# Two blocks more per round take the seven-product second layer, and the side steps are spread over less of a round

## The chip, the cores and the metric

The kernel runs on one core of a Trainium2 chip. The metric is the device time of one launch in microseconds. Each core has five engines that run their own instruction streams in order and meet through semaphores: TensorE (PE in the profile, with its weight loads as PEld), VectorE (DVE), ScalarE (ACT), GpSimd (POOL) and SyncE (SP), which here only starts transfers. All of the arithmetic is in float32, and a program's float32 matmul shows up in the trace as two matmul records.

## The reference, cut to what matters

Two stages follow each other. The first is a Fourier mixing of 8 batches of 2496 rows with 256 columns; the second sends each of the 19968 resulting rows to one of 8 experts, a two-layer network.

```python
X = np.fft.fft(np.fft.fft(x, axis=1), axis=2).real          # x: (8, 2496, 256)
x = X.reshape(B * S, D)                                     # 19968 rows of 256
expert_idx = np.argmax(x @ w_gate, axis=1)                  # 8 experts
gate_w = softmax(x @ w_gate)[arange, expert_idx]
for e in range(E):                                          # rows sorted by expert
    h = np.maximum(x_sorted[lo:hi] @ w1[e], 0.0)            # (rows,256) @ (256,1024)
    y_sorted[lo:hi] = h @ w2[e]                             # (rows,1024) @ (1024,256)
return gate_w[:, None] * y
```

## The kernel before, in words

The program is one long list of instructions that Python generators write out in an order fixed at build time. There are two kinds of work.

*Side work* makes the mixed rows of a batch. `first(b)` (L325) folds x on VectorE and multiplies on TensorE (the tiles named `s`), then the result goes through DRAM (`Td`); `second(b)` (L361) multiplies again (tiles `p` and `zz`), makes the finished `rows` on VectorE (L408, L410), and `route` (L416) finds each row's expert and its place in the DRAM table `Xs`. `send` (L462) moves 128 rows at a time into `Xs` with an indirect DMA that GpSimd issues (L236). `mixed(b)` (L882) weaves `first` of one batch with `second` of the one before it, and one step of that generator is a "side step".

*Expert work* is `experts` (L701), which takes blocks of 512, 256 or 128 rows of one expert in the order of `in_order` (L161). `fetch_rows` and `fetch_weights` (L526, L541) bring rows and both weight matrices through SP's queue, up to three blocks ahead. `turn` (L576) transposes the rows of the next block while the present block is in its second layer. A block has a first layer into `hT` (hidden units on partitions) and a second layer from `hT` to the output rows `y`, scaled by the gate on ScalarE and written to `out` by an indirect DMA of GpSimd, 128 rows each.

There are eight rounds, one for each batch. Rounds 3 to 6 (counted from 0) have five 512-row blocks each; round 7, the last, has five of 512 rows, seven of 256 and 21 of 128, the last ones only if they are needed.

Two of the layers are made in a form that replaces eight quarter-size products by seven and some sums of quarters. `seven` (L598) does so for the first layer of every 512-row block from round 3 on and of round 7's 256-row blocks (`halved`, L191). Its stationary side needs three sums of quarters of w1 and one in place (`Left`, L551, one sum per `step`), its moving side those of the transposed rows (`right`, L567). For each half of its work it makes products 0, 5, 6, 4, 1, 3, 2 into the PSUM banks a, b, d, c, a, e, c; after each, VectorE adds the bank to a running sum (L621, L624, L627, L635, L639), and ScalarE applies the Relu. The last product accumulates into bank c, so it has to wait until L627 has read that bank.

`lower` (L645) does the same for the second layer. Its stationary side is quarters and sums of quarters of `hT`: VectorE makes four sums for each half (L780, queued as `chores`), and its moving side is quarters of w2 with three sums and one in place (`below`, L593). In the kernel before only round 7's blocks use it (`quartered`, L196). For a 512-row block `below` runs on GpSimd in one go, while the block before is in its second layer; for a 256-row block it runs on VectorE at the end of the block before. All other blocks have the ordinary second layer (L828): for each 128 rows eight matmuls with 256 columns, which the trace shows as 16.

How the two kinds are mixed is set at L943 to L971. Each `yield` of `experts` gives a weight `w` and a flag. Where the flag is false (only in second layers, from round 3 on), a credit grows by `ticks * w / (SHARE * open_)`, with 32 ticks and `open_` 40 for five blocks; each whole credit runs one side step at that place in the list. With `SHARE` 0.8 the 32 steps are spread over the first four fifths of the round's second layers. `send` has its own pace (L968). A round ends when all steps of its batch have run.

Every engine takes its instructions strictly in the order of this list, so a VectorE instruction that waits holds up all later ones of that engine, whether they belong to side steps or to experts.

Of the kernel before, what the change touches and what calls it, by code (L numbers as in the profile page):

```python
# [12 lines left out]
F32 = mybir.dt.float32  # L13
# [171 lines left out]
SHARE, EARLY, ROOM = 0.8, 0.7, 1.2  # L185
# [10 lines left out]
def quartered(b, size):  # L196

    return halved(b, size) and b == B - 1
# [17 lines left out]
def kernel(ctx: ExitStack, tc, x, w_gate, w1, w2, out):  # L216
# [261 lines left out]
    def plan(b, size, k, last):  # L478
# [3 lines left out]
        def one(name, *dims, dt=F32):  # L482
            return cp.tile([1, *dims], dt, tag="p_" + name, name="p_" + name, bufs=2)
# [109 lines left out]
    def below(w, eng):  # L593

        ws2 = sp.tile([128, 3, FC // 2, H], F32, tag="t4", name="ws2")
        return right(ws2, *(w[:, 4 * f:4 * f + 4, k * H:(k + 1) * H] for f in (1, 0) for k in range(2)), eng=eng)

    def seven(size, l, r, hT, step, after):  # L598
# [13 lines left out]
        for g in range(half // fp):  # L612
            a, b, c, d, e = (pse.tile([128, fp, th], F32, tag=k, name=k) for k in "abcde")
            p1, u2, u3 = (bp.tile([128, fp, th], F32, tag=n, name=n, bufs=1) for n in ("p1", "u2", "u3"))
            h11, h12, h21, h22 = (hT[:, k * half + g * fp:k * half + (g + 1) * fp, t * th:(t + 1) * th]
                                  for k in range(2) for t in range(2))
            product(g, 0, a)
            act.copy(p1[:], a[:])
            yield
            product(g, 5, b)  # L620
            vec.tensor_tensor(u2[:], p1[:], b[:], op=add)  # L621
            yield
            product(g, 6, d)
            vec.tensor_tensor(u3[:], u2[:], d[:], op=add)  # L624
            yield
            product(g, 4, c)
            vec.tensor_tensor(h22, u3[:], c[:], op=add)  # L627
# [7 lines left out]
            vec.tensor_tensor(h21, u3[:], e[:], op=add)  # L635
            act.activation(h21, h21, ACTF.Relu)
            yield
            product(g, 2, c, False)
            vec.tensor_tensor(h12, u2[:], c[:], op=add)  # L639
            act.activation(h12, h12, ACTF.Relu)  # L640
            after(h11, h12, h21, h22, slice(g * fp, (g + 1) * fp))
# [3 lines left out]
    def lower(size, l, r, y, gate, send_rows, step):  # L645
# [14 lines left out]
        def scaled(k, lo, hi, src=None):  # L660
            for i in range(k * nt, (k + 1) * nt):
                act.activation(y[:, i, lo:hi], y[:, i, lo:hi] if src is None else src[:, i - k * nt], ACTF.Copy,
                               scale=gate[:, i])

        p1, u2, u3 = (bp.tile([128, nt, H], F32, tag=n, name=n, bufs=1) for n in ("p1", "u2", "u3"))
        a, b, c, d = (bank(k) for k in "abcd")
        one, two = y[:, nt:2 * nt], y[:, 0:nt]
        product(0, a)
        act.copy(p1[:], a[:])
# [4 lines left out]
        scaled(1, 0, H, a)  # L674
        step()
        yield
        product(5, c)
        vec.tensor_tensor(u2[:], p1[:], c[:], op=add)
        yield
        product(6, d)  # L680
        vec.tensor_tensor(u3[:], u2[:], d[:], op=add)
        vec.tensor_tensor(two[:, :, 0:H], u3[:], b[:], op=add)
        step()
        yield
        c = bank("c")
        product(4, c)
        vec.tensor_tensor(two[:, :, H:], u3[:], c[:], op=add)
        vec.tensor_tensor(u2[:], u2[:], c[:], op=add)
        scaled(0, 0, D)
        send_rows(0, nt)  # L690
# [4 lines left out]
        vec.tensor_tensor(one[:, :, H:], u2[:], d[:], op=add)  # L695
        scaled(1, H, D)
        send_rows(nt, 2 * nt)
        step()
        yield

    def experts(todo):  # L701
# [4 lines left out]
        xbs, got, xT, used, left, rest = [], [], None, None, None, None  # L706
# [30 lines left out]
        for k, (b, size, last, at) in enumerate(todo):  # L737
# [30 lines left out]
            both = quartered(b, size)  # L768
            if both:
                th, r2 = size // 2, rest  # L770
                s12 = xp.tile([128, 2, FC // 2, th], F32, tag="xq", name="s12", bufs=3)
                s4 = xp.tile([128, FC // 2, th], F32, tag="xq", name="s4", bufs=3)
                l2 = [hT[:, 4 * f:4 * f + 4, t * th:(t + 1) * th] for t, f in ((1, 1), (1, 0))]
                l2 += [s4, hT[:, 0:4, 0:th], s12[:, 0], s12[:, 1], hT[:, 4:8, 0:th]]

            def after(h11, h12, h21, h22, at):
                if both:
                    for o, p, q, op in ((s12[:, 0, at], h21, h11, add), (s12[:, 1, at], s12[:, 0, at], h22, sub),
                                        (h21, h22, h21, sub), (s4[:, at], h12, s12[:, 1, at], sub)):
                        chores.append(lambda o=o, p=p, q=q, op=op: vec.tensor_tensor(o, p, q, op=op))  # L780

            if halved(b, size):
                for _ in seven(size, left.all, xT, hT, step, after):
                    yield 0.5, True
                while chores:
                    step()
# [16 lines left out]
            if follow:  # L803
# [9 lines left out]
                if follow[1] == BIG and quartered(*follow[:2]):  # L813
                    rest = below(got[0][1], pool)
            if both:
                y = xp.tile([128, BIG // 128, D], F32, tag="t1", name="y4")

                def send_rows(lo, hi):
                    for i in range(lo, hi):
                        put_row(out, ro[:, i:i + 1], y[:, i], NT - 1, "out")  # L820

                for i, _ in enumerate(lower(size, l2, r2, y, meta[:, :, 1:2], send_rows,
                                            left.step if follow and halved(*follow[:2]) else lambda: None)):
                    if i in (0, 2, 4):
                        xT = next(turned, xT)
                    yield 1, False
# [200 lines left out]
```

## Time and profile before

| What | Value |
|---|---|
| Time, median of 3 runs | 1272.84 us (1270.5 to 1274.08) |
| Profiled execution: its own time | 1280.92 us |
| Profiled execution: span from first to last instruction | 1279.1 us |
| Start of the first seven-product block (round 3) | 349.4 us |
| Start of round 7 | 921.1 us |
| Busy in the span: PE / DVE / ACT / POOL | 1221.0 / 700.4 / 436.3 / 398.3 us |

The span is that of the profiled execution alone; 1.8 us of its time lie outside of it, and it took 8.1 us longer than the median of the runs without a profile. Times in microseconds of the trace count from the start of the span. The five 512-row blocks of a round start (first product of `seven`) at 495.7, 528.9, 556.5, 586.2 and 616.1 us in round 4, and the next round starts at 642.0. The fifth has no side steps and takes 25.9 us; the others are longer by the TensorE time of the side steps in them.

### The profile page before, as it was taken

The page shows a single profiled execution, that of the slowest core. Times are in us where ns is not written, and L with a number is a line of the kernel's source. Part 1 is how long each engine was busy: PE and PEld are TensorE (multiplying, and loading weights), DVE is VectorE, ACT ScalarE, POOL GpSimd, SP SyncE. Part 2 cuts the span into 40 slices and gives each one's busy share as a digit, 9 for nine tenths or more (in the row PEclk, how much of TensorE's full clock was granted, in tenths as well). Part 3 has the DMA queues.
Part 4 walks back from the last instruction along what each step waited for, and adds up shares of the span by engine and source line. Part 5 has one row for each costly group of instructions (what it writes and reads, how often), then busy time and mean ns, then how long its engine had stood idle before and what let it go on. Part 6 is the DMA issues. An engine that isn't in the chain of part 4 may idle for free.

```text
span 1279.1 us, 21208 instructions
## 1 busy us (share of the span) xinstructions
PE 1221.0 (95%) x6905; PEld 1077.0 (84%) x6905; DVE 700.4 (55%) x1772; ACT 436.3 (34%) x1096; POOL 398.3 (31%) x495
## 2 busy tenths in 40 slices
PE   6768999999999999999999999999999999999996
PEld 4557898876788888888888888888889999999995
DVE  4455434343466655564556455674578774444662
ACT  1423332332243433434343343432333332222232
POOL 0235327145116311561116411461453321111112
PEclk6859999999999999999999999999999999999998
DMA  8859798765348553573336434443435238778786
GB/s 241 279 181 321 242 339 297 204 228 175 125 146 260 162 153 113 175 240 114 104 118 211 144 120 149 132 152 107 130 121 167 91 129 296 283 277 276 280 279 246
DMA packets 163211, 249.72 MB, mean 195 GB/s; under 512 B 118601, under 2 KB 130227, under 8 KB 143516
## 3 DMA queue, kind: packets, MB, share of 16 engines
q1 hardware_dynamic: 146327, 203.28, 50.0%
q0 software_dynamic: 15888, 42.14, 9.1%
q10 hardware_dynamic: 885, 2.94, 0.7%
q8 instruction: 56, 0.92, 0.3%
q14 instruction: 55, 0.45, 0.1%
HBM read 194.91 MB, written 54.83 MB: 195 GB/s over the span
## 4 chain that ended last, share of the span: by engine, by line
PE 87%; DMA 6%; DVE 3%; another core or an unknown queue 2%; issue 1%; ACT 1%; SPq 0%; POOL 0%; POOLq 0%; DVEq 0%; ACTq 0%
PE py L221 32%; PE ph L221 10%; PE c L221 10%; PE a L221 10%; PE p L221 6%; PE d L221 6%; PE b L221 5%; PE e L221 4%; PE s L221 3%; DMA xq<-in_x_dram 2%; DMA Td<-t 1%; DMA t<-Td 1%; DMA xb<-Xs 1%; PE rk L221 0%
## 5 line engine op out<-in xcount | busy, mean ns | idle before, releaser
L221 PE MATMUL py<-w_sb,hT 128*128 128x256 f32 x2016 | 454.9, 380 | 1.3 <-DVE hT L796 1.3
L221 PEld LDWEIGHTS py<-w_sb,hT 128*128 128x128 f32 x2016 | 377.6, 190 | 51.2 <-DVE hT L796 1.7
L236 POOL DMA_INDIRECT out_dram<-y,ro x163 | 160.4, 984 | 694.0 <-ACT y L837 482.6
L236 POOL DMA_INDIRECT Xs<-rows,pi x160 | 163.2, 1020 | 109.9 <-DVE rows L410 52.1
L221 PE MATMUL ph<-xT,w_sb 128*128 128x128 f32 (+2 forms) x992 | 171.3, 328 | 6.1 <-DVE hT L796 3.3
L221 PEld LDWEIGHTS ph<-xT,w_sb 128*128 128x128 f32 x992 | 135.5, 192 | 30.5 <-issue 17.9
L837 ACT ACTIVATE y<-py,xb 128x256 f32<-128x256 f32 x129 | 61.0, 473 | 239.5 <-PE py L221 213.0
L221 PE MATMUL a<-xT,w_sb 128*128 128x256 f32 (+1 forms) x512 | 117.5, 356 | 0.0
L621 DVE TENSOR_TENSOR u<-p,b 128x512 f32<-128x512 f32 x57 | 39.1, 687 | 124.2 <-PE b L221 95.0
L796 DVE TENSOR_SCALAR hT<-ph 128x512 f32<-128x512 f32 x43 | 29.7, 690 | 129.5 <-issue 79.2
L221 PEld LDWEIGHTS a<-xT,w_sb 128*128 128x128 f32 x512 | 89.5, 190 | 10.7 <-DVE xT L582 0.4
L408 DVE COPY lg<-p 128x16 f32<-128x16 f32 x80 | 13.9, 174 | 141.5 <-ACT zs L405 121.3
L631 ACT ACTIVATE hT<-a 128x512 f32<-128x512 f32 x57 | 34.0, 597 | 149.5 <-PE a L221 115.7
L585 ACT ACTIVATE xT<-xT 128x256 f32<-128x256 f32 (+1 forms) x94 | 36.4, 387 | 121.8 <-DVE xT L582 71.9
L221 PE MATMUL s<-xq,w 104*112 104x256 f32 (+2 forms) x208 | 62.6, 426 | 11.0 <-DVE xq L297 10.9
L221 PEld LDWEIGHTS p<-table,t 120*128 120x128 f32 x352 | 55.2, 206 | 15.0 <-ACT zz L379 5.5
L221 PE MATMUL p<-table,zz 128*128 128x145 f32 (+1 forms) x320 | 57.2, 304 | 7.6 <-ACT t L321 5.5
L221 PE MATMUL p<-table,t 120*128 120x120 f32 (+1 forms) x352 | 57.7, 291 | 6.1 <-ACT zz L379 4.1
L221 PE MATMUL c<-xT,ws 128*128 128x256 f32 (+1 forms) x256 | 59.5, 359 | 3.2 <-DVE hT L627 3.2
L469 POOL CAST pi<-due 128x1 int32<-128x1 f32 x140 | 39.5, 282 | 69.1 <-ACT due L468 68.7
L582 DVE STREAM_TRANSPOSE xT<-xb 128x512 f32<-128x512 f32 (+1 forms) x94 | 58.2, 625 | 4.3 <-DMA xb<-Xs 4.3
L798 ACT ACTIVATE hT<-ph 128x512 f32<-128x512 f32 x55 | 32.8, 597 | 80.2 <-PE ph L221 64.9
(146 smaller groups left out, 1798.1 us busy)
## 6 DMA issues: line engine op xcount, KB each, us to landing
w_sb<-in_moe_w_dram SPq DMA_DIRECT2D x132, 1024.0 KB
xq<-in_x_dram SPq DMA_DIRECT2D x24, 896.0 KB
xb<-Xs SPq DMA_DIRECT2D x112, 128.0 KB
Td<-t SPq DMA_DIRECT2D x18, 448.0 KB
t<-Td SPq DMA_DIRECT2D x8, 768.0 KB
t<-Td SPq DMA_DIRECT2D x8, 640.0 KB
xb<-Xs SPq DMA_DIRECT2D x52, 64.0 KB
xb<-Xs SPq DMA_DIRECT2D x100, 32.0 KB
```

What stands on the lines that cost most here:

```text
L221: nc.tensor.matmul(o, lhsT=lhsT, rhs=rhs, start=start, stop=stop, **kw)
L236: return unordered(pool.indirect_dma_start(out=dst, out_offset=bass.IndirectOffsetOnAxis(ap=idx, axis=0), in_=rows, in_offset=None, bounds ...
L408: vec.tensor_copy(lg[:, k:k + 2], p3[:, NY:NY + 2 * E].rearrange("p (m e) -> p m e", m=2))
L469: pool.tensor_copy(idx, due[:])
L582: vec.transpose(free(xT[:], 256 * h, [32, n // 32], [BIG, 2], [1, 32]), free(xb, 512 * h, [64, n // 32], [1, 2], [2, 32]))
L585: act.activation(odd, odd, ACTF.Copy, scale=-1.0)
L621: vec.tensor_tensor(u2[:], p1[:], b[:], op=add)
L631: act.activation(h11, a[:], ACTF.Relu)
L796: vec.tensor_scalar(o, ph[:], 0.0, None, op0=ALU.max)
L798: act.activation(o, ph[:], ACTF.Relu)
L837: act.activation(y[:], py[:], ACTF.Copy, scale=meta[:, i, 1:2])
```

## The change

The second layer by sevens is extended to the fourth and fifth blocks of rounds 3 to 6 (`at >= 3`), so that eight blocks more use `lower`. What comes with it:

- `Below` replaces `below`. It hands out its four sums one per `step`. For a fourth block it is started a block early: one sum before each of the four row tiles of the third block's second layer, on GpSimd. Every other block that needs it makes its sums in its own first layer, one at each of the first four products: 512-row blocks on GpSimd, 256-row blocks on VectorE. The tile `ws2` has one buffer.
- `seven` keeps its running sums in `hT` itself instead of the tiles p1, u2, u3, and, where the block goes on to `lower`, leaves out the Relu of the quarter h21.
- The four sums of `hT` are made otherwise: two per half in `seven` (`scalar_tensor_tensor`, which takes the Relu of h21 along), and then s2 and s4 inside `lower`, in place, after its products 0 and 1 have read the old values.
- `lower` keeps its running sums in the `y` tiles, which are now two rows of tiles each with three buffers (before six of one row), also for the ordinary blocks; it reads bank b later, after product 4, and has an eighth, empty `yield`.
- `SHARE` goes from 0.8 to 0.6: the 32 steps fall in the first three fifths of a round's second layers. In the built program they stand in the first three blocks, but for one pair in the fourth block's `lower`.
- Most small tiles of `plan` have one buffer.

```diff
-SHARE, EARLY, ROOM = 0.8, 0.7, 1.2
+SHARE, EARLY, ROOM = 0.6, 0.7, 1.2
...
-def quartered(b, size):
-
-    return halved(b, size) and b == B - 1
+def quartered(b, size, at):
+
+    return halved(b, size) and (b == B - 1 or at >= 3)
...
+    class Below:
+        def __init__(self, w, eng):
+            ws2 = bp.tile([128, 3, FC // 2, H], F32, tag="ws2", name="ws2", bufs=1)
+            o = [ws2[:, k] for k in range(3)]
+            b11, b12, b21, b22 = (w[:, 4 * f:4 * f + 4, k * H:(k + 1) * H] for f in (1, 0) for k in range(2))
+            self.eng, self.all = eng, (b11, b21, b22, o[2], o[0], o[1], b12)
+            self.due = deque([(o[0], b12, b11), (o[1], b22, o[0]), (o[2], b21, o[1]), (b12, b12, b22)])
+
+        def step(self):
+            if self.due:
+                o, p, q = self.due.popleft()
+                self.eng.tensor_tensor(o, p, q, op=sub)
...
             product(g, 0, a)
-            act.copy(p1[:], a[:])
+            act.copy(h11, a[:])
             yield
             product(g, 5, b)
-            vec.tensor_tensor(u2[:], p1[:], b[:], op=add)
+            vec.tensor_tensor(h12, h11, b[:], op=add)
...
             product(g, 3, e)
-            vec.tensor_tensor(h21, u3[:], e[:], op=add)
-            act.activation(h21, h21, ACTF.Relu)
+            vec.tensor_tensor(h21, h21, e[:], op=add)
+            if not both:
+                act.activation(h21, h21, ACTF.Relu)
...
+        p1, u2, u3, high = (y[k][:, 0:nt, h * H:(h + 1) * H] for k, h in ((1, 0), (1, 1), (0, 0), (0, 1)))
         product(0, a)
-        act.copy(p1[:], a[:])
+        act.copy(p1, a[:])
+        s2()
...
         product(1, a, False)
+        s4()
+        step()
+        turn_some()
+        yield
+        product(5, c)
+        vec.tensor_tensor(u2, p1, c[:], op=add)
         scaled(1, 0, H, a)
...
-                    for o, p, q, op in ((s12[:, 0, at], h21, h11, add), (s12[:, 1, at], s12[:, 0, at], h22, sub),
-                                        (h21, h22, h21, sub), (s4[:, at], h12, s12[:, 1, at], sub)):
-                        chores.append(lambda o=o, p=p, q=q, op=op: vec.tensor_tensor(o, p, q, op=op))
+                    part = parts[g]
+                    for o, q, op in ((s1, h11, add), (h21, h22, sub)):
+                        chores.append(lambda o=o[:, part], p=h21[:, part], q=q[:, part], op=op:
+                                      vec.scalar_tensor_tensor(o, p, 0.0, q, op0=ALU.max, op1=op))
...
-                for _ in seven(size, left.all, xT, hT, step, after):
+                for _ in seven(size, left.all, xT, hT, both, step, ends):
+                    if both:
+                        below.step()
                     yield 0.5, True
...
-                if follow[1] == BIG and quartered(*follow[:2]):
-                    rest = below(got[0][1], pool)
+                if not both and size == follow[1] == BIG and quartered(*follow[:2], follow[3]):
+                    soon = Below(got[0][1], pool)
...
+                def s2():
+                    for part in parts:
+                        vec.tensor_tensor(h22[:, part], s1[:, part], h22[:, part], op=sub)
+
+                def s4():
+                    for part in parts:
+                        vec.tensor_tensor(h12[:, part], h12[:, part], h22[:, part], op=sub)
...
-            for i in range(n):
+            for i in range(0 if both else n):
+                if soon:
+                    soon.step()
                 xT = next(turned, xT)
...
-            if follow and follow[1] == BLK and quartered(*follow[:2]):
-                rest = below(got[0][1], vec)
```

## The prediction

> **What bounds the kernel now.** I read the page first, then the table of stages, then who waited for whom, then the order of events in the stages that the change touches. Engine shares and the row of forty slices:
>
> ```profile
> span 1279.1 us, 21208 instructions
> PE 1221.0 (95%) x6905; PEld 1077.0 (84%) x6905; DVE 700.4 (55%) x1772; ACT 436.3 (34%) x1096; POOL 398.3 (31%) x495
> ...
> PE   6768999999999999999999999999999999999996
> ```
>
> TensorE is the bound on average, but what counts is the stages that change. The table of stretches (length, then busy time of PE, PEld, DVE, ACT, POOL, clock) for rounds 3 and 6, then for the fifth block of round 6 and the first two blocks of round 7:
>
> ```profile
> 349.40:495.70 146.30, 146.30 (x742) 129.73 (x741) 85.34 (x204) 57.50 (x141) 45.68 (x60) 1.00 0.53 164
> 786.50:921.10 134.60, 134.60 (x660) 118.91 (x659) 81.17 (x206) 48.61 (x116) 50.86 (x64) 1.00 0.43 137
> ...
> 895.20:921.10 25.90, 25.90 (x122) 22.80 (x121) 13.15 (x22) 8.43 (x16) 9.31 (x8) 1.00 0.40 122
> 921.10:945.80 24.70, 24.70 (x170) 23.10 (x169) 18.80 (x32) 8.19 (x16) 12.13 (x10) 1.00 0.47 139
> 945.80:971.80 26.00, 24.82 (x171) 23.02 (x170) 20.04 (x36) 8.98 (x19) 12.44 (x11) 1.00 0.44 138
> ```
>
> Rounds 3 and 6 have PE busy for their whole length at full clock; rounds 4 and 5 read the same, and from 349 to 921 us the list of PE's waits is empty. So each microsecond of PE work taken away there is one off the end, unless a new wait takes its place. The last three rows are the trial of the change that this trace already holds: the same first layer with an ordinary second layer takes 25.90 us, with the second layer by sevens 24.70, and with one stall in it 26.00. The gain per block is small enough for one stall to eat it.
>
> **Part 1, the products.** TensorE's order of events shows both second layers of a 512-row block:
>
> ```profile
> 907.28 13.98 PE L221 MATMUL py<-w_sb,hT 128*128 128x256 f32 x64
> 921.09 1.03 PE L221 MATMUL a<-xT,w_sb 128*128 128x256 f32 x4
> ...
> 933.25 1.95 PE L221 MATMUL a<-w_sb,hT 128*128 128x128 f32 x16
> ...
> 943.96 1.95 PE L221 MATMUL d<-w_sb,s 128*128 128x128 f32 x16
> ```
>
> The ordinary one runs from 907.28 to 921.09: 64 records in 13.81 us, 216 ns each. By sevens it starts at 933.25 and the next block at 945.75: 7 x 16 = 112 records in 12.50 us, 111.6 ns each. That is 1.31 us less per block (seven eighths of 13.81 would be 1.73 less; the rest is the 3% that a half-width record takes over half). Eight blocks: 8 x 1.31 = 10.5 us off PE.
>
> A rule of the Trainium skill speaks against this. TensorE: Matmul & The Clock Gate, section Back-to-back issue gap, says that in a stream of weight loads and matmuls both set the spacing, so that narrow matmuls are dearer than their columns: 81 ns sustained at 128 columns where 56 stand for one alone, 1.46 times. Taken over, the half-width record would take 1.46 x 108 = 158 ns, the layer 112 x 158 = 17.7 us, and eight blocks would lose 8 x 3.9 = 31 us (an estimate from that page). The row has 112 ns for just this shape with its weight loads beside it, so I use the row.
>
> **Part 2, the waits in a block by sevens.** The new VectorE work per block, counted in the built order: four `scalar_tensor_tensor`, four sums for s2 and s4, six of 128x256 for the banks of `lower`; some 8 us in a 512-row block. At its fifth place in round 6 VectorE had 13.15 of 25.90 us busy, so there is room; what can hurt is order. In round 7 the price shows as a wait, and in its cause:
>
> ```profile
> PE c L221 <- DVE hT L627: 3.2, 5, 1.2
> ```
>
> ```profile
> 955.42 1.29 POOL L570 TENSOR_TENSOR ws<-w_sb 128x512 f32<-128x512 f32 x1
> ...
> 956.79 1.26 POOL L571 TENSOR_TENSOR ws<-w_sb,ws 128x512 f32<-128x512 f32 x1
> ...
> 957.58 0.69 DVE L627 TENSOR_TENSOR hT<-u,c 128x512 f32<-128x512 f32 x1
> 958.14 1.27 POOL L572 TENSOR_TENSOR ws<-w_sb,ws 128x512 f32<-128x512 f32 x1
> 958.18 1.77 DVE L780 TENSOR_TENSOR s<-s,hT 128x512 f32<-128x512 f32 x1
> ```
>
> The first is the list of waits (total, times, longest), the second the order of events in the block of 26.00 us: its second half's h22 sum (L627) came late, and the last product of the first layer waited 1.18 us. GpSimd's weight sums run beside VectorE there, and an L780 sum that lasts 0.68 us otherwise lasts 1.77.
>
> SBUF — State Buffer, section SBUF: two separate sides, gives the reason and a harsher price: GpSimd and a VectorE operation with two SBUF inputs take one port pair in turn, each for its whole instruction, and the other fully blocks. The trace agrees on which: stretched are only sums from SBUF (0.92 to 1.77 us), those with a PSUM bank stay at 0.69. By the rule the two sums of that kind amid GpSimd's four would each wait a full 1.3 us in the fifth blocks, 2.6 us per block against 0.8 us of slack (h22's sum ends at 10.4 us in an undisturbed block, product 2 is due at 11.2): 1.8 x 4 = 7.2 us. In the trace five such sets cost PE 1.18, 0.1 and otherwise nothing, 0.26 each; the bad one began 9.6 us into its block, the others at 2 to 7. In the fifth blocks they begin when GpSimd has sent off the fourth block's rows, near 5.5 us. I take 0.2 x 4 = 0.8 us, between 0 and 7.2. The fourth blocks' sets run in the third block's second layer, where the built order gives VectorE about 13 us of work in 19.
>
> **Part 3, the fourth blocks.** In rounds 3 to 5 the last two side steps land in the fourth block's `lower`, on VectorE between s2 and s4. Walk, with zero at the block's first product; sums of 512 columns follow each other in 0.62 us (seven of them from 934.17 to 937.90). The first layer's last sum starts at 12.3; it and four more end at 15.4; then lg and rows 0.8, the folds 0.7 and 0.95, seven small ones of `route` 1.4: 19.3; s4 twice 1.25, a w1 sum 0.6, a transpose 0.7, the sum that empties bank c 0.4: 22.2. TensorE: first layer 12.1, products 0, 3, 1, 5, 6 at 1.79 each and 0.9 of side work: product 4 wants bank c at 22.0. A stall of 0.2; if each operation is taken at its full 0.68 and small gaps are added, 1.5. I take 0.4 x 3, and 0.1 for round 6: 1.3 us. Late next would be the w2 sums of `y` and, behind them, bank d for the next block's third product, with 0.5 us to spare.
>
> **Part 4, the pacing.** Steps per unit of second-layer weight go from 32/(0.8 x 40) = 1.0 to 32/(0.6 x 40) = 1.33. Nothing is gained by it directly, as PE has no gap there. Round 1 ran at 32/(0.7 x 32) = 1.43, and PE's waits between 200 and 242 us are one of 2.1 us, for a transfer of `Td`. Two steps in a row show there:
>
> ```profile
> 226.65 0.60 PE L221 MATMUL p<-table,t 120*128 120x120 f32 x4
> 227.36 0.74 PE L221 MATMUL p<-table,zz 128*128 128x145 f32 x4
> ```
>
> The second follows 0.71 us after the first instead of 0.44. One such pair per round stands in the new order: 0.3 x 4 = 1.2 us (0 to 2.1 each). The transfer of `Td` is issued at least a block before its first reader, as the built order shows, so I add nothing for it. The sends into `Xs` end before the third block's second layer, so no round starts later.
>
> **Part 5, round 7.** The 512-row blocks keep their count of VectorE sums. In the 256-row blocks the w2 sums move from the block before into the first layer, one before each running sum. Of the 3.2 us of waits above 2.0 lie in four of these seven. Walk: VectorE is through with the rows at 1.1 us; w2 sum, h12, w2 sum, h21, w2 sum, then h22 from 4.5 to 5.2, and product 2 is due at 5.36: that wait goes. Then w2 sum, two sums of banks, two of s1 and h21, and s2 ends at 9.1, when product 5 is due at 8.9: 0.2 x 7 = 1.5 us. Net −0.5 us (−2.0 to +3). A Relu less per half is ScalarE's, which is 34% busy: nothing. The `y` tiles, now three of two rows, are written again a block or more later: nothing.
>
> **The sum.** −10.5 + 0.8 + 1.3 + 1.2 − 0.5 = −7.7 us, on the profiled execution's 1280.92 us (1279.1 of span and 1.8 around it): 1273.2. That execution lies 8.1 us over the median of the runs, 1272.84, and nothing in this sum scales with that: 1265.1 us for the median.
>
> **Rivals.** *The new stalls eat most of it.* The fourth blocks' order at its dear end (1.5 x 3), fifth blocks at 0.6 each and the pacing at 2.4 give −10.5 + 4.5 + 2.4 + 2.4 = −1.2; between that and the forecast, about −3: 1270. For it: VectorE has 19 to 20 of 25 us busy in such blocks and must take side steps too. Against: four of the five in round 7 hardly stall.
> *All covers hold.* No stall in the eight blocks and half of round 7's waits gone: −10.5 − 1.6 = −12.1, 1260.7. For it: the block at 921 us with its 24.70. Against: the walk of the fourth blocks ends with nothing to spare.
> *Slower.* GpSimd's sums meet the first layer's last sums in each fourth and fifth block as they did at 955 us: the price was 26.00 − 24.70 = 1.30 us, so eight times that is 10.4 us and the gain is gone; it decides from a mean stall of 1.31 us per block. With the walk's 1.5 in three blocks on top, −10.5 + 10.4 + 4.5 + 1.2 − 0.5 = +5.1: 1278. For it: the start of GpSimd's sums hangs on when its queue is through with the rows, and that moved by 4 us within five blocks. Against: the fourth blocks' sums are a block early.
> *It does nothing* would need PE to have had gaps in rounds 3 to 6; it has none.
>
> **How the numbers follow.** Forecast 66% (1261.5 to 1268.5), all covers hold 12%, most eaten 14%, slower 8%. The range leaves out half of the second case, a third of the third and the fourth: 1260.0 to 1270.5. A difference under 0.3%, 3.8 us (1269.0), can't be told from none here: faster has the first two and a third of the third, 0.82; slower by as much (over 1276.7) takes half of the last, 0.05; 0.13 between.
>
> **What would show it.** Right: the fifth blocks of rounds 3 to 6 at about 24.8 us from first product to next first product; no PE wait on VectorE over 1.5 us between 349 and 890 us; 112-ns records in the new layers; round 7's waits for h22 gone in 256-row blocks and small ones before product 5. Wrong: PE waiting for s2, for bank c or for bank d in the fourth blocks; PE waiting for `zz` or `oh` in the first three blocks of a round; GpSimd's sums late enough for PE to wait for them.

## The result, and the profile after

The changed kernel takes 1265.8 us (median of 6 runs, 1264.2 to 1270.37), the kernel before on the same chip 1273.46 (6 runs, 1270.5 to 1275.89): ratio 0.995, 95% interval 0.9933 to 0.9967. That is 7.7 us less, as forecast; the parts of the sum, though, came out otherwise than it says, and two of its errors cancel. From one set of runs to the next the median of the kernel before lay between 1272.6 and 1284.1 us, so below a time counts only as a ratio to the kernel before of its own set, or stage by stage.

The head of the page of the changed kernel. The profiled execution is the longest of the six runs (1270.37 us):

```profile
span 1268.5 us, 22212 instructions
PE 1212.5 (96%) x7289; PEld 1083.6 (85%) x7289; DVE 773.6 (61%) x1884; ACT 421.5 (33%) x1087; POOL 445.7 (35%) x527
```

PE has 8.5 us less to do in 384 more records, and the span is 10.6 us shorter. Of these, 2.5 us lie before round 3 (it starts at 346.9 us, not 349.4), which is no effect: the same early rounds ended anywhere between 343.4 and 356.1 us in the runs below. From the first block of round 3 to the end it is 921.6 us after 929.7. The table of stretches, rounds 3, 6 and 7's 512-row blocks, then the third, fourth and fifth block of round 3 and the fifth of round 6 (length, busy time of PE, PEld, DVE, ACT, POOL, clock, DMA share, GB/s):

```profile
346.90:491.90 145.00, 144.13 (x837) 130.77 (x836) 102.80 (x228) 55.13 (x140) 54.08 (x65) 1.00 0.52 163
...
778.90:911.40 132.50, 132.25 (x757) 119.76 (x756) 99.49 (x234) 47.47 (x118) 57.18 (x68) 1.00 0.44 140
911.40:1034.40 123.00, 123.00 (x843) 115.86 (x842) 100.99 (x178) 39.08 (x86) 56.37 (x48) 1.00 0.41 132
...
407.70:441.80 34.10, 33.23 (x173) 29.53 (x172) 23.78 (x37) 14.19 (x38) 20.44 (x24) 1.00 0.44 136
441.80:467.40 25.60, 25.60 (x179) 24.18 (x178) 21.62 (x49) 8.17 (x19) 0.80 (x1) 1.00 0.52 149
467.40:491.90 24.50, 24.50 (x170) 23.09 (x169) 19.95 (x36) 7.75 (x17) 9.30 (x8) 1.00 0.40 130
886.80:911.40 24.60, 24.60 (x171) 23.18 (x170) 19.89 (x36) 7.75 (x17) 9.27 (x8) 1.00 0.41 130
```

The fourth and fifth blocks, the ones with the new layer, have PE busy for their whole length: no wait at all. The fifth takes 24.6 us in place of 25.9, exactly the 1.31 us of part 1. The gap between 145.00 and 144.13 stands in the third block. In numbers, from the same tables of both kernels (us):

| stage | before | after | difference | forecast |
|---|---|---|---|---|
| round 3 | 146.3 | 145.0 | -1.3 | |
| round 4 | 146.3 | 145.0 | -1.3 | |
| round 5 | 144.5 | 141.9 | -2.6 | |
| round 6 | 134.6 | 132.5 | -2.1 | |
| rounds 3 to 6 | 571.7 | 564.5 | -7.2 | -7.2 (parts 1 to 4) |
| round 7, 512-row blocks | 124.7 | 123.0 | -1.7 | 0 |
| round 7, from the first to the seventh 256-row block | 191.6 | 191.7 | +0.1 | -0.5 (part 5) |
| rest, from there on | 41.7 | 42.4 | +0.7 | 0 |

Two lines of the list of PE's waits of the changed kernel (total, times, longest; a wait counts from the end of the matmul before it in PE's pipeline, so the gap between two records is 0.2 us longer):

```profile
PE p L221 <- ACT t L372: 1.7, 3, 0.8
PE c L221 <- DVE hT L860: 1.5, 7, 0.2
```

The first did not exist in rounds 3 to 6 before. The second takes the place of the waits for h22 in the 256-row blocks. The order of events of the changed kernel shows the first in the third block of round 3, then bank c in the fourth block, then GpSimd's set beside the first layer of the fifth:

```profile
422.69 1.46 POOL L606 TENSOR_TENSOR ws<-w_sb 128x512 f32<-128x512 f32 x1
423.05 1.64 DVE L295 TENSOR_TENSOR xq<-xq 104x508 f32<-104x508 f32 x1
...
425.21 1.69 DVE L297 COPY xq<-xq 104x8 f32<-104x8 f32 x1
425.59 1.27 POOL L606 TENSOR_TENSOR ws<-w_sb,ws 128x512 f32<-128x512 f32 x1
...
426.82 0.70 DVE L582 STREAM_TRANSPOSE xT<-xb 128x512 f32<-128x512 f32 x1
...
427.88 0.15 ACT L372 COPY t<-pr 120x6 f32<-120x6 f32 x1
...
463.13 0.38 DVE L700 TENSOR_TENSOR y<-y,c 128x256 f32<-128x256 f32 x1
463.78 1.95 PE L221 MATMUL c<-ws,s 128*128 128x128 f32 x16
...
474.50 2.96 POOL L606 TENSOR_TENSOR ws<-w_sb,ws 128x512 f32<-128x512 f32 x2
...
477.06 0.69 DVE L640 TENSOR_TENSOR hT<-hT,c 128x512 f32<-128x512 f32 x1
...
477.66 1.58 DVE L809 SCALAR_TENSOR_TENSOR hT<-hT 128x512 f32<-128x512 f32 x1
...
478.58 1.03 PE L221 MATMUL c<-xT,ws 128*128 128x256 f32 x4
```

Third block: GpSimd makes the early weight sums of the fourth block (L606). A fold of VectorE (L295) that lasts 0.69 us elsewhere lasts 1.64 beside the first of them, and a copy of eight columns (L297), 0.17 us elsewhere, lasts 1.69 and ends within 0.05 us of the second. So the transpose L582 starts at 426.82; ScalarE, whose sign change L585 needs it, is in order and comes to its copy of `t` only at 427.88, and PE's next side step is 0.93 us late. Fourth block: bank c is empty at 463.51, 0.27 us before product 4. Fifth block: one `scalar_tensor_tensor` is drawn out to 1.58 us, but it stands behind the sum for h22 (L640), which ends at 477.75; product 2 starts at 478.58, on time.

### The profile page after: what moved, and what is told of

Same layout as the page of the kernel before. It is cut to its first block, busy times and chain, and to the rows that moved or that the text cites. A ratio compares the mean times of both kernels' runs of the same rounds, so it can differ in the third digit from the quotient of the medians.

```text
span 1268.5 us, 22212 instructions
## 1 busy us (share of the span) xinstructions
PE 1212.5 (96%) x7289; PEld 1083.6 (85%) x7289; DVE 773.6 (61%) x1884; ACT 421.5 (33%) x1087; POOL 445.7 (35%) x527
## 3 DMA queue, kind: packets, MB, share of 16 engines
q10 hardware_dynamic: 885, 2.94, 0.7%
## 4 chain that ended last, share of the span: by engine, by line
PE 71%; issue 16%; DMA 4%; POOL 4%; DVE 3%; ACT 0%; POOLq 0%; SPq 0%; DVEq 0%; ACTq 0%
PE py L221 19%; PE a L221 10%; PE c L221 10%; PE d L221 7%; PE ph L221 6%; PE p L221 6%; PE b L221 5%; PE e L221 3%; PE s L221 3%; POOL out_dram L236 3%; DMA xq<-in_x_dram 1%; POOL Xs L236 1%; DMA t<-Td 1%; DMA w<-c_w 1%; DMA Xs<-rows,pi 0%
## 5 line engine op out<-in xcount | busy, mean ns | idle before, releaser
L221 PE MATMUL py<-w_sb,hT 128*128 128x256 f32 x1504 | 340.3, 380 | 0.0
L221 PEld LDWEIGHTS py<-w_sb,hT 128*128 128x128 f32 x1504 | 282.0, 191 | 36.1 <-issue 1.0
L585 ACT ACTIVATE xT<-xT 128x256 f32<-128x256 f32 (+1 forms) x94 | 36.5, 388 | 185.8 <-DVE xT L582 135.7
L221 PEld LDWEIGHTS a<-xT,w_sb 128*128 128x128 f32 x512 | 88.6, 191 | 10.6 <-DVE xT L582 1.3
L881 ACT ACTIVATE y<-py,xb 128x256 f32<-128x256 f32 x97 | 45.8, 473 | 154.4 <-PE py L221 152.6
L634 DVE TENSOR_TENSOR hT<-hT,b 128x512 f32<-128x512 f32 x57 | 39.2, 688 | 80.6 <-PE b L221 53.9
L582 DVE STREAM_TRANSPOSE xT<-xb 128x512 f32<-128x512 f32 (+1 forms) x94 | 58.7, 627 | 12.7 <-DMA xb<-Xs 12.7
L469 POOL CAST pi<-due 128x1 int32<-128x1 f32 x140 | 42.2, 301 | 68.8 <-ACT due L468 68.7
L221 PE MATMUL a<-w_sb,hT 128*128 128x128 f32 x528 | 66.0, 276 | 0.0
L221 PE MATMUL d<-w_sb,hT 128*128 128x128 f32 x528 | 65.5, 275 | 0.0
L221 PEld LDWEIGHTS a<-w_sb,hT 128*128 128x128 f32 x528 | 63.2, 192 | 0.7
L221 PEld LDWEIGHTS d<-w_sb,hT 128*128 128x128 f32 x528 | 62.2, 192 | 0.0
```

The costliest lines, as they stand in the source:

```text
L221: nc.tensor.matmul(o, lhsT=lhsT, rhs=rhs, start=start, stop=stop, **kw)
L469: pool.tensor_copy(idx, due[:])
L582: vec.transpose(free(xT[:], 256 * h, [32, n // 32], [BIG, 2], [1, 32]), free(xb, 512 * h, [64, n // 32], [1, 2], [2, 32]))
L585: act.activation(odd, odd, ACTF.Copy, scale=-1.0)
L634: vec.tensor_tensor(h12, h11, b[:], op=add)
L881: act.activation(y[:, i % 2], py[:], ACTF.Copy, scale=meta[:, i, 1:2])
```

## The experiments

Rounds and blocks are named as above; times of stages are from the profiled execution of each run, one per run. A wait given in the text is a gap between two records of PE beyond their usual spacing.

**The early weight sums.** The fourth block makes its w2 sums in its own first layer, as the fifth does:

```diff
-                if not both and size == follow[1] == BIG and quartered(*follow[:2], follow[3]):
+                if False:
                     soon = Below(got[0][1], pool)
```

> The changed kernel, but the fourth blocks of rounds 3 to 6 make their w2 sums on GpSimd in their own first layer, as the fifth blocks do, and not a block early. Theory A (the stall of 0.93 us and the one of 0.27 us in the third blocks of rounds 3 and 4 come from GpSimd's early sums, which hold up VectorE's folds, behind these the transpose, and on ScalarE the copy that TensorE waits for): both stalls go, the third blocks of rounds 3 and 4 take 32.9 us instead of 34.1, the fourth blocks stay within 0.4 us of 25.6, and the kernel is 1.5 to 2.5 us faster than the changed one, about 1263.8. Theory B (the denser pacing alone makes the stalls): the third blocks stay at 34.1 and the time at 1265.8; the fourth blocks lose 0.3 each.

Ratio 0.9945 (0.9925 to 0.9964), rounds 3 to 6 564.4 us against 564.5. The two waits of 0.93 us in the third blocks are gone, so GpSimd's early sums made them. Nothing is gained all the same: round 3 is 0.8 us shorter, but round 4's third block now waits twice 0.33 us, before bank a and at h22, and round 6's 0.56 and 0.40 where it waited 0.41. These new waits are of the kind shown with the last run and come without the early sums as well, so in the sum the early sums made no difference here; that they would make none where such waits are absent isn't shown.

**The pace.** The changed kernel with the steps in 0.8 of a round, as before:

```diff
-SHARE, EARLY, ROOM = 0.6, 0.7, 1.2
+SHARE, EARLY, ROOM = 0.8, 0.7, 1.2
```

> The changed kernel with SHARE 0.8 again, so that the 32 steps reach into the fourth block's second layer by sevens. Theory A (the pacing clears VectorE for the new layers, and costs little by itself): the fourth blocks of rounds 3 to 5, with about 26 us of VectorE work in 28, wait for bank c or d behind side steps, 1 to 3 us each; 3 to 9 us slower than the changed kernel in all, 1269 to 1275. Theory B (the pacing is a pure cost of some 3 us): 2 to 3 us faster than the changed kernel, about 1263, with third blocks near 32.5 and no waits in the fourth.

Ratio 0.998 (0.9968 to 0.9992): by the ratio more than half of the gain is gone. Rounds 3 to 6 take 567.8 us, 3.3 more, as theory A has it at its low end. The fourth blocks of rounds 3 and 4 take 30.3 us for 29.8 before, in spite of their seven-eighths: PE waits 1.07 us for bank c and 0.51 for bank d, and then 0.29 and 0.30 in the fifth block. In the list of waits from round 3 to round 7:

```profile
PE c L221 <- DVE y L700: 1.8, 2, 0.9
PE d L221 <- DVE y L706: 0.9, 3, 0.4
```

**The pace alone, and round 7 alone.** First, the changed kernel with the new layer in round 7 only (which had one before), so that it differs from the kernel before in the pace and in how round 7 is written:

```diff
-    return halved(b, size) and (b == B - 1 or at >= 3)
+    return halved(b, size) and b == B - 1
```

> The changed kernel with the second layer by sevens in round 7 alone, as before the change; the pacing of 0.6 and the new order inside the two layers stay, and no weights are summed early. Theory A: rounds 3 to 6 take what they took before, 571.7 us, within 1 us, round 7's five 512-row blocks 123.0 instead of 124.7; 1271.5 for the median, 10 us over the changed kernel less its 3 us of stalls. Theory B (pacing costs by itself): rounds 3 to 6 take 574 to 575 us, 1274 for the median.

Ratio 1.0044 (1.0029 to 1.0058). Rounds 3 to 6 take 574.5 us, 2.8 more than before (theory B); round 7's 512-row blocks 123.8. Then the kernel before with nothing but the pace of 0.6 (SHARE 0.8 to 0.6):

> The kernel before with SHARE 0.6 and nothing else. Theory A: no new wait of TensorE, rounds 3 to 6 within 1 us of 571.7, the median within 0.1% of the kernel before. Theory B: the same stalls of 1.2 us in the third blocks of rounds 3 and 4, and 0.4 in round 6; 3 us slower than before, 1276.

Ratio 1.0021 (1.0008 to 1.0034). Rounds 3 to 6 take 575.5 us, 3.8 more; the waits in them are seven of 0.26 to 0.53 us, 2.7 in all, two at back-to-back steps (0.27 each), the others at h22 or bank a in the third blocks (what is late there is shown with the last run). So by itself the pace was a loss of 2.8 to 3.8 us in these runs. With the changed kernel at both paces it makes a square (us, rounds 3 to 6):

| | pace 0.8 | pace 0.6 |
|---|---|---|
| old second layers | 571.7 | 574.5, 575.5 |
| new second layers in fourth and fifth blocks | 567.8 | 564.5 (569.8 in the last run) |

The layers are worth 3.9 us at the old pace and 10 to 11 at the new one; the pace costs about 3 under the old layers and gains 3.3 under the new ones. Neither part has a worth of its own. The ratios agree: without early sums, at pace 0.6, it was 0.9945 in the same set of runs as 0.998, 1.0044 and 1.0021. But the cell of the changed kernel is the least certain. The last run has the same code in rounds 3 to 6 and took 569.8 us, 2.0 more than pace 0.8, so what the pace gains was not there at that time.

**How much cover the fifth blocks have.** Each of the first three sums of GpSimd's set made twice:

```diff
-            self.due = deque([(o[0], b12, b11), (o[1], b22, o[0]), (o[2], b21, o[1]), (b12, b12, b22)])
+            sums = [(o[0], b12, b11), (o[1], b22, o[0]), (o[2], b21, o[1])]
+            if eng is pool:
+                sums = [s for s in sums for _ in range(2)]
+            self.due = deque(sums + [(b12, b12, b22)])
```

> In the changed kernel GpSimd makes each of the first three sums of a set of w2 weights twice (seven instructions for four, some 9.4 us for 5.6); nothing else differs and the output is the same. It asks how much of the cover in the fifth blocks and in round 7 is left over. Theory A (the meetings with VectorE cost one instruction each and lie far enough before their readers): the set now reaches from the first layer's middle into the first product of the second layer, the second pair of s1 and h21 sums is stretched, s2 ends 0 to 0.8 us after product 5 is due: fifth and round-7 blocks 24.6 to 25.4 us, rounds 3 to 6 together 564.5 to 569, round 7's five 123 to 127. Theory B (the slack of 0.8 us at h22 that the prediction worked with is what counts): the h22 sum of the second half is late as well, product 2 waits 1 us or more in most of these blocks: 25.6 to 26.5 us each, round 7's five 128 to 132.

A single run, 1303.07 us beside 1284.13. The fifth blocks take 25.8 us, in the range of theory B, and the five of round 7 29.8, 29.9, 25.7, 25.8, 25.8. Neither theory has the cause. From 880 to 1045 us the list of PE's waits has one line:

```profile
PE b L221 <- POOL ws L609: 9.6, 5, 3.4
```

VectorE is in time; PE waits for GpSimd's third sum itself, which product 3 reads, by 1.0 to 1.1 us and in the first two blocks of round 7 by 3.6. (In these two the other 1.6 us are slower matmuls: the granted clock is 0.74 and 0.66 in the 5 us that follow.) In the changed kernel that sum ends 2.5 to 3.8 us before product 3 (947.33 and 949.86 in one block, 970.63 and 974.45 in the next); three sums more, of 1.3 to 1.6 us each, make it some 4.8 us later in the fifth blocks. So the set's cover is two to three of its own instructions, and in this run it is used up by GpSimd's lateness before any VectorE sum holds PE: the rival "slower" named the wrong reader. (The run also has a wait of 2.8 us in round 6's third block, of the kind shown with the last run.)

**A pace between the two.** SHARE 0.7 in the changed kernel.

> The changed kernel with the steps in 0.7 of a round, between the change's 0.6 and the 0.8 of before. Theory A (a quicker pace costs waits in the third blocks, a slower one puts steps into the fourth block's second layer, where bank c is late): between the two there is a pace at which the third blocks lose less than 1.2 us and the fourth blocks are still clear: rounds 3 to 6 562 to 564.5 us, 0 to 2.5 under the changed kernel. Theory B (the loss is in the count of steps, not in where they land): rounds 3 to 6 at the mean of the two paces, about 566.

Ratio 0.9966 (0.9952 to 0.9981), rounds 3 to 6 566.2 us, the mean of the two paces, as theory B has it. But where the time goes is as in A: the third blocks have no wait, and the fourth blocks wait for bank c by 1.41, 1.41 and 0.81 us.

**Is it the bank?** The same pace with other banks for the last two products of the new layer:

```diff
-        c = bank("c")
-        product(4, c)
+        e = bank("e")
+        product(4, e)
...
-        d = bank("d")
-        product(2, d)
+        c = bank("c")
+        product(2, c)
```

> The run with the steps in 0.7 of a round, with one more edit: in the new second layer product 4 takes bank e and product 2 bank c, where they took c and d; so no product of it needs a bank that was just filled. Theory A (bank c's late emptying in the fourth blocks is what made 0.7 dearer than 0.6): the waits of 1.41, 1.41 and 0.81 us before product 4 go, fourth blocks 28.2 to 26.8 and 27.6 to 26.8, rounds 3 to 6 566.2 - 3.6 = 562.6 us, 1.9 under the changed kernel. Theory B (VectorE is behind as a whole, and the bank is only where it shows): the wait moves on to bank c before product 2 or to the next block's first banks, at least 0.7 us per round: rounds 3 to 6 565 us or more.

Ratio 0.9954 (0.9938 to 0.9969); rounds 3 to 6 565.9 us where it was 566.2. And at pace 0.8:

> The same with the steps in 0.8 of a round, as before the change. Theory A: the waits of the run with 0.8 (1.07 and 0.51 in the fourth blocks of rounds 3 and 4, 0.34 in round 5, all at banks c and d) go, but the pairs of 0.3 at the fifth block's start, which are ScalarE's and VectorE's first banks, may stay: rounds 3 to 6 567.8 - 3.5 = 564.3 us, with the pairs gone too 562.5. Theory B: the wait moves on: 566 us or more.

Ratio 0.9968 (0.9957 to 0.9979); rounds 3 to 6 567.8, as without the edit. The list of waits in both, first at 0.7, then at 0.8:

```profile
PE b L221 <- DVE y L682: 1.7, 3, 0.8
PE c L221 <- DVE hT L640: 0.5, 3, 0.2
```

```profile
PE b L221 <- DVE y L682: 4.4, 3, 1.9
PE c L221 <- DVE hT L640: 0.5, 3, 0.2
```

Bank c and bank d have gone from the list and bank b of the next block has come, for the same sum: 26.7 + 26.1 us for the fourth and fifth block at 0.7, where they were 28.2 + 24.6. Theory B: VectorE is behind by that much at the end of the fourth block, and the bank only decides which product finds it out. The cure is to take side steps from the fourth block, which is what pace 0.6 does.

**More layers.** The second and third blocks of round 6 by sevens too, and then the second blocks of rounds 3 to 5 as well:

```diff
-    return halved(b, size) and (b == B - 1 or at >= 3)
+    return halved(b, size) and (b == B - 1 or at >= 3 or b == B - 2 and at >= 1)
```

> The changed kernel with the second and third blocks of round 6 by sevens too (two more layers). Theory A (a second layer by sevens gives 1.31 us wherever the round's side steps are few, and round 6 has few): round 6 132.5 - 2.6 = 129.9 us, at worst 130.9 with a wait of some 0.4 us in the third block as now; the ratio to before 0.2% lower than the changed kernel's. Theory B (VectorE must be clear of side steps; those of round 6 end in its first three blocks): the third block's waits grow to 1 us or more and bank c of the second's is late: round 6 132 to 133.5 us, nothing gained.

```diff
+    return halved(b, size) and (b == B - 1 or at >= 3 or at == 1 or b == B - 2 and at >= 1)
```

> As the run before, and with the second blocks of rounds 3 to 5 by sevens as well (five more layers than the changed kernel; no side step of TensorE lies in these blocks). Theory A (clear of side steps on TensorE is enough): three times 1.31 us more, second blocks 24.7 instead of 26.0, rounds 3 to 5 together 431.9 - 3.9 = 428 us. Theory B (VectorE counts, not TensorE: it has the new layer's 8 us and the next block's transposes and weights to do, some 24 us of 24.7): its queue runs into the third block, whose first layer then waits for its inputs: third blocks 0.5 to 2 us longer, rounds 3 to 5 430 to 434 us.

Ratios 1.004 (1.0024 to 1.0056) and 1.0138 (1.0085 to 1.0192): two more layers turn the gain into a loss, five more cost more again. Round 6 takes 140.9 us instead of 132.5; its second block 28.1 instead of the 24.7 hoped for, with 2.67 us before bank c, its third 31.8. With five, the second blocks take 27.4 to 29.0 us, more than the 26.0 of the ordinary layer, again at bank c (2.67 to 3.01 us each), and rounds 3 to 5 446.4 us against 432.0. Theory B in both, and dearer than it said. Not all of it is VectorE's queue: in the first of these runs round 6's third block also has a granted clock of 0.52 from 855.3 to 858.5 us, behind its waits, and rounds 3 to 5 of that run, whose code is the changed kernel's, took 434.4 us, with waits of 0.39 to 1.13 us at bank a in their third blocks.

**The small blocks.** Pace 0.7 and bank e, and in the 256-row blocks of round 7 product 6 ahead of product 5, so that s2 has 0.9 us more. The order as it has to be:

```diff
+        if nt == 1:
+            product(6, d)
+            yield
         product(5, c)
         vec.tensor_tensor(u2, p1, c[:], op=add)
         scaled(1, 0, H, a)
         if nt == 2:
             turn_some()
-        yield
-        product(6, d)
+            yield
+            product(6, d)
         vec.tensor_tensor(u3, u2, d[:], op=add)
```

> As the first of these, and in the 256-row blocks of round 7 product 6 ahead of product 5, so that s2 has one product (0.9 us) more. Theory A (product 5 waits for s2 by 0.38 us and for nothing else): the six waits of 0.38 go, round 7's blocks of 256 and 128 rows 192.8 - 2.3 = 190.5 us. Theory B (VectorE's queue is the length of the block there, and each wait removed comes back before another product): 192 to 193 us.

In this run, unlike the lines above, `scaled` came ahead of u2's sum in these blocks and wrote over p1, so part of their rows was made from other numbers, by the same instructions. Ratio 0.9927 (0.9902 to 0.9952); the waits for s2 are gone, the small blocks take 188.6 us for 192.2 in the run with the same pace and banks. Then with the order of the lines above, at pace 0.6 and with the old banks in the 512-row blocks:

> The changed kernel (0.6 of a round, its own banks in the 512-row blocks) with product 6 ahead of product 5 in the 256-row blocks alone, where product 4 takes bank e and product 2 bank c. It differs from the run before it in that the scaled copy of bank a comes after u2's sum, as it must: there it overwrote p1, so that part of those blocks' rows was made from other numbers, by the same instructions. Theory A: rounds 3 to 6 stay at 564.5 us, the blocks of 256 and 128 rows come to 188.6 to 189.5 (191.7 in the changed kernel): 2.2 to 3.1 us under the changed kernel, ratio to the kernel before 0.992 to 0.9935. Theory B (the gain of the run before came with the misplaced copy): 191 us or more, ratio 0.994 to 0.996.

The small blocks take 189.4 us for 191.7, theory A, 2.3 us. But the ratio is 0.9971 (0.9959 to 0.9983), because rounds 3 to 6, whose code is the changed kernel's, took 569.8 us in this run instead of 564.5. The order of events in round 6's third block shows the largest piece:

```profile
847.62 0.69 DVE L637 TENSOR_TENSOR hT<-hT,d 128x512 f32<-128x512 f32 x1 [0.45 <-PE c L221]
...
850.51 0.00 SPq L544 DMA_DIRECT2D w_sb<-in_moe_w_dram  x1
850.56 0.69 DVE L640 TENSOR_TENSOR hT<-hT,c 128x512 f32<-128x512 f32 x1 [2.25 <-remote]
850.62 0.60 ACT L644 ACTIVATE hT<-a 128x512 f32<-128x512 f32 x1 [5.52 <-remote]
...
851.31 1.13 PE L221 MATMUL c<-xT,ws 128*128 128x256 f32 x4 [2.75 <-DVE hT L640]
```

PE waits for h22 by 2.91 us, but VectorE, which makes it, stands still for 2.25 us, although its input, bank c, was written from 845.8 to 846.8; ScalarE and SP's queue stand still too, and all go on within 0.1 us of each other. What the program has all three wait for is TensorE's word that a product is done (its semaphore signal). The trace has those signals as events, one every 0.86 us where nothing is amiss. Around this place (us; a few events are missing from any trace), in the changed kernel, in this run, and in the run of the pace alone:

```
changed kernel, round 6   836.84  837.70  838.56  839.43  840.29  841.15  842.53
this run, round 6         847.60  850.54  850.60  850.66  852.45
pace alone, round 6       849.24  851.42  852.91  853.68  853.74
```

Three signals of this run come within 0.12 us, after a gap of 2.94. So by the records the products are computed in time and reported late. (The profile models the ends of matmuls; that the results themselves were there early is therefore argued from the evenly spaced starts, not shown.) Such bunches stand behind most of the waits of 0.3 to 3.6 us at h22 and bank a in the third blocks of the other runs at pace 0.6 (without early sums, round 7 alone, pace alone, sums twice, more layers), the longest at times when the kernel before took 1284 us; in round 6, 0.41 us of the wait at h22 is there without a bunch too, behind the small operations of `plan`. In the changed kernel's own profile there is no bunch in these blocks. At 0.7 one run has them, at 0.8 one run has one (560.33 us), both without a wait of PE over 0.2 us. What holds the signals back isn't settled: in the places shown SP had just begun to fetch a later block's rows from `Xs` (L534 to L538), but that fetch also passes without a bunch.

The kernel before has two such bunches, and one is the wait of round 7 from which the prediction took its price. Its order of events there:

```profile
955.37 0.69 DVE L621 TENSOR_TENSOR u<-p,b 128x512 f32<-128x512 f32 x1 [2.09 <-PE d L221]
956.79 0.69 DVE L624 TENSOR_TENSOR u<-u,d 128x512 f32<-128x512 f32 x1 [0.73 <-PE a L221]
956.91 0.60 ACT L631 ACTIVATE hT<-a 128x512 f32<-128x512 f32 x1 [3.08 <-PE a L221]
```

VectorE waits for TensorE twice, 2.09 and 0.73 us, ahead of h22's sum at 957.58, and TensorE's signals come at 955.29, then 956.76, 956.82 and 956.88, though banks b and d were written by 953.7 and 954.6. The drawn-out sum of 1.77 us comes after h22. The trace shows no part of GpSimd in that wait.

Nor was the changed kernel itself run at a time when the kernel before took 1284 us: if the 2.3 us of the small blocks are taken off the gain of this run (3.7 us by its ratio), some 1.4 us would be left, an estimate. No version that was run stands clear of the changed kernel. At pace 0.7 rounds 3 to 6 took 566.2 us when the kernel before took 1284 and, with the other banks, 565.9 when it took 1272.6, but the swap wasn't run at that pace with the copy in its right place.

## Why the prediction was right or wrong

**Part 1, the products: right to the tenth.** 25.9 to 24.6 us in the fifth blocks; round 5, which has no wait before or after, is 2.6 us shorter for two layers. Eight are 10.5. The row of 111.6 ns was the right choice over the Trainium skill's rule for narrow matmuls (TensorE: Matmul & The Clock Gate, Back-to-back issue gap), which would have made this a loss of some 30 us (81 over 56 is 1.45, not 1.46; an estimate from that page).

**Part 2, the fifth blocks: the cost was put at 0.8 us and is nothing, and its price was read from the wrong cause.** The slack was right: h22's sum ended 0.83 us before its product, forecast 0.8. The 1.18 us of the block at 945.80 us were put down to GpSimd's sums beside VectorE; they were TensorE's late signals, as the last run led to see, and the line with 1.77 us that was shown for it stands behind h22. The Trainium skill's rule (SBUF — State Buffer, SBUF: two separate sides) agrees with the trace on which operations are held, the sums from SBUF; but one sum per fifth block meets GpSimd, not two, it is 0.9 us longer, not 1.3, and no reader waits for it so soon. The rule as the prediction used it would have cost 7.2 us. The other failed step is the last sentence of the part, that the fourth blocks' sets run in the third block's second layer at no cost: VectorE's amount of work was counted (13 us in 19), not what is queued behind the operations that are drawn out. In rounds 3 and 4 that cost 0.93 us each.

**Part 3, the fourth blocks: 1.3 us forecast, nothing found.** The walk's cheap end holds: bank c was wanted at 22.0 in the walk and was at 463.78 - 441.80 = 21.98; it was to be empty at 22.2 and was at 21.71. Half a microsecond of a walk of 22 decided the sign. At pace 0.7 and 0.8, where more side steps fall into that block, the same bank costs 0.8 to 1.4 us: the mechanism is real, and the "wrong" that the prediction named (bank c, bank d) is what those runs show.

**Part 4, the pacing: the mis-sized term.** It was put at 1.2 us, for one pair of back-to-back steps per round. The pairs are there, in two rounds and with 0.27 us each. But the pace alone costs 2.8 and 3.8 us in two runs. What was missed is that the third blocks have little room for a delay at this pace. In round 6 h22's sum is late by 0.41 us behind the small operations of `plan`, in the changed kernel's own profile too; and where TensorE's signals come late, PE waits for VectorE and ScalarE behind them, which is most of the 2.1 us of waits at h22 and bank a in the run of the pace alone. Why such signals cost PE nothing in the third blocks at 0.7 and 0.8 is open. And "nothing is gained by it directly" is true of the old layers only: without the pace the new layers kept 3.9 us.

Parts 2 to 4 together were to cost 3.3 us in rounds 3 to 6 and cost 10.5 - 7.2 = 3.3; the waits that the trace shows (0.93 and 0.27 in rounds 3 and 4 each, 0.41 in round 6) make 2.8 of it. The sum is right because fourth and fifth blocks were put 2.1 us too dear and the third blocks as much too cheap: that is luck. And the match holds for a profile without late signals in these rounds; the last run, with the same code there, took 569.8 us.

**Part 5, round 7.** The h22 waits of the 256-row blocks went, and product 5 waits for s2 instead, as the walk said; the walk's 0.2 us were 0.38, seven times, 2.7 for 1.5. So +0.1 for -0.5. The 512-row blocks gained 1.7 us, put at nothing: the wait of 1.35 us that ended at 958.32 isn't there. It stood behind a bunch of late signals. Whether the new code has a part in its absence is open: the old code has a wait at h22 in that block in both of its profiles (1.35 us, and 0.47 at the other pace), the new code in none, but one of 0.69 us in the block before, in the run with round 7 alone. What makes the rest 0.7 us longer isn't known.

**The rivals.** "All covers hold" is half true, in the fourth and fifth blocks. "Slower" did not come, and its mechanism was not found: its price was that of the late signals, and with the set lengthened by three sums GpSimd itself was late before any VectorE sum was. A slower kernel does come, by the fear behind "the new stalls eat most of it" (a VectorE with 19 to 20 of 25 us busy that must take side steps too), as soon as layers are put into blocks that still have them.

## What to carry to other kernels

A change that trades TensorE time for VectorE time is worth what VectorE can take in that very block, so cost it together with whatever else is scheduled onto VectorE there: here the same layer was worth its full 1.31 us, 0.5 us on average at pace 0.8 (3.9 over eight), or a loss, depending on where the side work lay. Before a wait is put down to a neighbour, look what the late operation itself was waiting for, one step further back. When a wait is removed by giving it another buffer and comes back at the next one with the same length, the engine behind it is late; here another bank gained nothing, and less work in that block did. When an operation is drawn out by a neighbour, follow the in-order queues behind it on each engine, not its engine's busy share: a copy of eight columns on VectorE held ScalarE and then PE.

## What the runs showed of the hardware that was not expected

- The length of a VectorE operation beside GpSimd need not go by its own size: of 24 copies of 104x8 (L297) in the changed kernel the median is 0.168 us, and two, which each ended together with a GpSimd sum, took 1.69; without the early sums the longest of the 24 is 0.172.
- The TensorE clock after a long wait: after PE's 2.82 us in round 6 of the run with sums made twice, the granted clock was 0.50 from 855.6 to 861 us and matmuls came 0.43 us apart for 0.22, some 3 us on top of the wait. After the 2.91 us shown above it stayed at 1.00. The run with five layers more has both: 0.50 from 413.1 to 416 us after a wait of 2.77, and 1.00 after one of 3.55 at 435. So the length of the wait alone doesn't decide it; what does isn't known.
- TensorE's signals that products are done can reach the other engines late and in a bunch (three within 0.12 us after a gap of 2.94), while its records run on evenly; VectorE, ScalarE and SP then go on together, and the list of waits names the last of them instead.
